# The first FFN product of chunks 2 to 8 by Strassen's scheme, with every operation of chunks 1 to 8 in a planned order

## The chip, the cores and the metric

The kernel runs on one core of one Trainium2 chip. The metric is the time of one execution in device microseconds, as a median over runs. Engines are named as in the profile: PE is TensorE (matmuls; PEld its weight loads), DVE is VectorE, ACT is ScalarE, POOL is GpSimd, SP is SyncE, which issues the DMA transfers.

## The reference

Attention over pooled keys and values, then a feed-forward network (FFN) with PReLU. There are 8 batches and 8 heads of 576 queries with 64 dimensions; keys and values are averaged over groups of 8, so 72 of each are left. The result is 4608 tokens of 512 features.

```python
k_p = k.reshape(B, H, Sp, pool, D).mean(axis=3)
v_p = v.reshape(B, H, Sp, pool, D).mean(axis=3)
scores = scale * np.matmul(q, k_p.transpose(0, 1, 3, 2))
scores = scores - np.max(scores, axis=-1, keepdims=True)
attn = np.exp(scores)
attn = attn / (np.sum(attn, axis=-1, keepdims=True) + 1e-09)
attn_out = np.matmul(attn, v_p)
...
h = x @ w_in
g = np.maximum(h, 0.0) + alpha * np.minimum(h, 0.0)
return (g @ w_out).astype(np.float32)
```

Here w_in is 512 x 2048 and w_out 2048 x 512.

## The kernel before

**Tiling.** The 4608 tokens are worked on in nine chunks of 512 (CH), numbered 0 to 8 here. A chunk has an attention part (`attention`) that makes its x, 512 features by 512 tokens, and an FFN part. Every fp32 operand of a matmul is split into a high and a low float16 part, and a product is the sum of three matmuls (low x high, high x low, high x high), which is why three lines stand side by side: L763 to L765 in the first FFN product, L810 to L812 in the second.

**The FFN of a chunk.** The first product (`ffn1_products`) makes 16 slices f of 128 hidden features each: 4 feature blocks of x times 3 matmuls of 128 x 128 weights and 512 columns, in one PSUM bank. Then ScalarE scales the slice from PSUM to SBUF (`ffn1_scaled`, L769), VectorE applies the PReLU (`ffn1_prelu`, L773; from chunk 1 on it reads SBUF alone, in chunk 0 it reads PSUM too), and the slice g is split: ScalarE writes the high part (L781) and GpSimd the low part (L784). The second product (`ffn2`) takes 128 tokens at a time: 16 slices times 3 matmuls of 512 columns in one bank, an output copy on ScalarE (L800) and a store on SP (L805). In the last tile of the last chunk the bank is made in two halves of 256 columns.

**The attention of a chunk.** Loads of q, k and v; group sums of k on VectorE (L374) and of v on GpSimd (three halvings, L461); maxima for the scales; splits of k, q and v; then for each of four tiles of 128 tokens: the scores on PE (L596), maximum and subtraction on VectorE (L505, L519), the exponential on ScalarE (L522), sum and reciprocal on VectorE, the product with the reciprocal on GpSimd (L530), the high part on ScalarE (L539, into a padded buffer `apad`), a copy of it by DMA (L536), two low parts on GpSimd (L542, L545) and a DMA transpose into `aT` (L550). After the four tiles the product with v, called mix (L606), gives x, which is split on ScalarE and VectorE (L564, L568).

**The order.** Chunk 0, the preparation of the weights and the attention of chunk 1 are ordered by `_Plan`: every operation is added with an engine, a duration, the operations that it needs, a rank and the buffers that it takes and gives, and `emit` writes out, again and again, the operation with the best rank among those that its engine could start soonest. From chunk 1 on the FFN operations are written down in a loop (L917 to L935), the attention of the next chunk is cut into portions that go between the 16 slices (`_Line`), and the Tile framework orders them. Buffers rotate: PSUM has two banks for slices (`ps_h`), two for outputs (`ps_o`) and two pairs for scores, mix and maxima (`ps_s`); in SBUF `fp` has four, `wp` three exponent buffers, `apads` two.

Of the kernel before, what the change touches and what calls it, by code (L numbers as in the profile page):

```python
# [7 lines left out]
F16 = mybir.dt.float16  # L8
# [24 lines left out]
LO0 = P - SP  # L33
TINY = 2.0 ** -100
# [38 lines left out]
class _Plan:  # L73

# [11 lines left out]
    def __init__(self, fill, **room):  # L86
        self.fill = fill
        self.ops, self.room, self.port = [], {k: n * [0.0] for k, n in room.items()}, 0.0

    def add(self, engine, us, emit, *after, rank=0.0, take=None, give=None, two=False):  # L90
        op = dict(engine=engine, us=us, emit=emit, after=after, rank=rank, n=len(self.ops),
                  take=take, give=(give,) if isinstance(give, str) else give or (), end=None,
                  two=two or engine == "Pool")
        self.ops.append(op)
        return op

    def start(self, op, free):
        if any(d["end"] is None for d in op["after"]) or (op["take"] and not self.room[op["take"]]):
            return None
        t = [free.get(op["engine"], 0.0)] + [d["end"] for d in op["after"]]  # L100
        if op["take"]:
            t.append(min(self.room[op["take"]]))
        if op["two"]:
            t.append(self.port)
        return max(t)

    def emit(self):
        free, left = {}, list(self.ops)
        while left:
            best = {}  # L110
            for op in left:
                t = self.start(op, free)
# [3 lines left out]
            for ready in best.values():  # L116
                t0 = min(t for t, _ in ready) + self.NEAR[ready[0][1]["engine"]]
                picks.append(min((x for x in ready if x[0] <= t0), key=lambda x: (x[1]["rank"], x[1]["n"])))
# [9 lines left out]
            if op["take"]:  # L128
                self.room[op["take"]].remove(min(self.room[op["take"]]))
            for kind in op["give"]:  # L130
                self.room[kind].append(op["end"])
            op["emit"]()
            left.remove(op)
# [3 lines left out]
def pooled_attention_prelu_ffn(ctx: ExitStack, tc: tile.TileContext, qT, kT, vT, kN, vN, w1, w2, alpha, out):  # L137
# [13 lines left out]
    atp = ctx.enter_context(tc.tile_pool(name="atp", bufs=1))  # L151
    xp = ctx.enter_context(tc.tile_pool(name="xp", bufs=4))
    fp = ctx.enter_context(tc.tile_pool(name="fp", bufs=ROOM["f"]))
    wp = ctx.enter_context(tc.tile_pool(name="wp", bufs=ROOM["e"]))
    gp = ctx.enter_context(tc.tile_pool(name="gp", bufs=16))
    ps_s = ctx.enter_context(tc.tile_pool(name="ps_s", bufs=2, space=PSUM))
    ps_h = ctx.enter_context(tc.tile_pool(name="ps_h", bufs=2, space=PSUM))
    ps_o = ctx.enter_context(tc.tile_pool(name="ps_o", bufs=2, space=PSUM))

    kbs = [const.tile([P, NPR, 2, SP], F16, name=f"kb{i}") for i in range(2)]  # L160
    apads = [const.tile([P, 2, H, P], F16, name=f"apad{i}") for i in range(2)]
    for i in range(2):
# [6 lines left out]
    nc.gpsimd.affine_select(out=ident, in_=ident, compare_op=ALU.not_equal, fill=1.0, base=0,  # L169
                            pattern=[[-1, P]], channel_multiplier=1)  # L170
# [21 lines left out]
    def reduce_max(add, r, m, n, *after, narrow=False, cap=None, rank=0.0):  # L192
# [7 lines left out]
        ps = once(lambda: ps_s.tile([P, 2, CH], F32, tag="s", name="pm"))  # L200
# [22 lines left out]
        return add("DVE", 0.4 + 0.13 * n, lambda: (maxima(), clamp()), *xs_, rank=rank, give="S")  # L223
# [78 lines left out]
    def attention(add, c, bs, rank, begin=False, early=False, k_pool=0, q_cuts=1, on_act=(), on_dve=(), behind=()):  # L302
# [99 lines left out]
        if first:  # L402
# [4 lines left out]
            def alpha_scales():  # L407
# [6 lines left out]
                nc.vector.tensor_scalar(out=xsc, in0=xsc, scalar1=2.0 ** -26, scalar2=None, op0=ALU.mult)  # L414
# [78 lines left out]
        for i in range(TPC):  # L493
# [40 lines left out]
            for l in range(2):  # L534
                if l and c > 1:
# [94 lines left out]
    def picked(f, n, of=NF):  # L630

        return (f + 1) * n // of > f * n // of
# [335 lines left out]
```

## Time and profile before

| | us |
|---|---|
| median of 3 runs | 872.73 (871.78 to 873.32) |
| the profiled execution's own time | 871.06 |
| its span, first to last instruction | 869.0 |
| PE busy in the span | 832.5 (96%) |
| DVE, ACT, POOL busy | 422.4, 408.8, 367.2 |

The profile is of one execution. Busy time counts instructions of an engine as the profiler sees them. Matmuls are pipelined: each is listed with 0.38 us, but the next one starts before it has ended, so what one costs is the distance between two starts. A row of the timeline has the start, the duration, the engine, the line of the program and, in square brackets, how long the engine was idle before and what ended that. A row of line groups has the busy time, the mean duration in ns, and the idle time before the group's instructions with what ended it.

### The profile page before, as it was taken

The page shows a single profiled execution, that of the slowest core. Times are in us where ns is not written, and L with a number is a line of the kernel's source. Part 1 is how long each engine was busy: PE and PEld are TensorE (multiplying, and loading weights), DVE is VectorE, ACT ScalarE, POOL GpSimd, SP SyncE. Part 2 cuts the span into 40 slices and gives each one's busy share as a digit, 9 for nine tenths or more (in the row PEclk, how much of TensorE's full clock was granted, in tenths as well). Part 3 has the DMA queues.
Part 4 walks back from the last instruction along what each step waited for, and adds up shares of the span by engine and source line. Part 5 has one row for each costly group of instructions (what it writes and reads, how often), then busy time and mean ns, then how long its engine had stood idle before and what let it go on. Part 6 is the DMA issues. An engine that isn't in the chain of part 4 may idle for free.

```text
span 869.0 us, 12499 instructions
## 1 busy us (share of the span) xinstructions
PE 832.5 (96%) x4941; PEld 397.1 (46%) x4941; DVE 422.4 (49%) x649; ACT 408.8 (47%) x692; POOL 367.2 (42%) x371
## 2 busy tenths in 40 slices
PE   6779899989999999999999999999999999999998
PEld 5444344434444444444444444444444444444445
DVE  4889995476129511872176208820782055112210
ACT  5999993545324531554155324632453255213330
POOL 0358473278215820683067406731573047103320
PEclk9999999999999999999999999999999999999999
DMA  9687042604710551047004701381126005100000
GB/s 341 228 249 293 26 105 51 206 4 78 202 52 5 100 179 43 13 84 196 30 23 74 210 25 28 64 196 48 28 55 146 13 20 94 36 25 13 1 24 25
DMA packets 122905, 78.92 MB, mean 91 GB/s; under 512 B 106176, under 2 KB 107008, under 8 KB 122848
## 3 DMA queue, kind: packets, MB, share of 16 engines
q1 hardware_dynamic: 122848, 78.14, 33.2%
q8 instruction: 38, 0.62, 0.3%
q14 instruction: 19, 0.16, 0.1%
HBM read 45.10 MB, written 9.44 MB: 63 GB/s over the span
## 4 chain that ended last, share of the span: by engine, by line
PE 70%; DVE 15%; ACT 6%; issue 3%; DMA 3%; POOL 2%; SPq 1%; ACTq 0%; POOLq 0%; DVEq 0%
PE o L810 13%; PE o L812 12%; PE o L811 12%; PE h L763 9%; PE h L764 9%; PE h L765 9%; DVE t L773 4%; DVE q L440 2%; PE x L606 2%; ACT t L769 2%; DMA qraw<-qT_dram 1%; PE idle L841 1%; DMA nat<-kN_dram 1%; POOL e L530 1%; DVE pr L215 1%
## 5 line engine op out<-in xcount | busy, mean ns | idle before, releaser
L784 POOL TENSOR_TENSOR g<-t,g 128x512 f16<-128x512 f32 x144 | 172.1, 1196 | 322.8 <-ACT g L781 322.8
L773 DVE SCALAR_TENSOR_TENSOR t<-t,al 128x512 f32<-128x512 f32 x128 | 127.1, 994 | 267.4 <-ACT t L769 259.3
L763 PE MATMUL h<-x,w 128*128 128x512 f16 x576 | 219.1, 380 | 11.7 <-ACT t L769 7.3
L764 PE MATMUL h<-x,w 128*128 128x512 f16 x576 | 219.0, 380 | 1.2 <-DVE x L568 1.1
L765 PE MATMUL h<-x,w 128*128 128x512 f16 x576 | 218.8, 380 | 0.0
L810 PE MATMUL o<-w,g 128*128 128x512 f16 (+1 forms) x560 | 208.1, 373 | 1.7 <-POOL g L784 0.9
L811 PE MATMUL o<-w,g 128*128 128x512 f16 (+1 forms) x560 | 208.8, 373 | 0.0
L812 PE MATMUL o<-w,g 128*128 128x512 f16 (+1 forms) x560 | 205.9, 373 | 0.0
L781 ACT CAST g<-t 128x512 f16<-128x512 f32 x144 | 88.6, 616 | 103.2 <-DVE t L773 102.8
L769 ACT ACTIVATE t<-h,rp 128x512 f32<-128x512 f32 x144 | 97.9, 681 | 68.6 <-PE h L765 60.6
L800 ACT ACTIVATE o<-o,os 128x512 f32<-128x512 f32 x33 | 22.5, 687 | 171.0 <-PE o L812 171.0
L764 PEld LDWEIGHTS <-w 128*128 128x128 f16 x576 | 56.4, 98 | 76.4 <-issue 14.7
L810 PEld LDWEIGHTS <-g 128*128 128x128 f16 x592 | 57.9, 98 | 68.7 <-POOL g L784 1.8
L812 PEld LDWEIGHTS <-g 128*128 128x128 f16 x592 | 57.9, 98 | 66.5
L461 POOL TENSOR_TENSOR vraw<-vraw 72x512 f32<-72x512 f32 (+1 forms) x56 | 56.4, 1023 | 75.3 <-DMA vraw<-vT_dram 66.6
L811 PEld LDWEIGHTS <-g 128*128 128x128 f16 x592 | 57.9, 98 | 66.0 <-issue 1.3
L765 PEld LDWEIGHTS <-w 128*128 128x128 f16 x576 | 56.5, 98 | 68.9 <-issue 2.6
L763 PEld LDWEIGHTS <-w 128*128 128x128 f16 x576 | 56.4, 98 | 65.5 <-issue 0.8
L568 DVE SCALAR_TENSOR_TENSOR x<-x,xsc,x 128x512 f16<-128x512 f32 x36 | 25.9, 748 | 79.1 <-ACT x L564 79.1
L530 POOL TENSOR_TENSOR e<-e,sm 128x576 f32<-128x576 f32 x35 | 43.8, 1252 | 21.9 <-DVE sm L528 20.7
L542 POOL TENSOR_TENSOR apad<-e,apad 128x448 f16<-128x448 f32 x36 | 39.2, 1090 | 8.1 <-ACT apad L539 8.1
L539 ACT CAST apad<-e 128x576 f16<-128x576 f32 x44 | 28.8, 669 | 22.9 <-POOL e L530 11.8
(131 smaller groups left out, 741.3 us busy)
## 6 DMA issues: line engine op xcount, KB each, us to landing
w<-w_dram SPq DMA_DIRECT2D x16, 1024.0 KB
out_dram<-o SPq DMA_DIRECT2D x35, 256.0 KB
qraw<-qT_dram SPq DMA_DIRECT2D x17, 512.0 KB
vraw<-vT_dram SPq DMA_DIRECT2D x28, 288.0 KB
kraw<-kT_dram SPq DMA_DIRECT2D x12, 576.0 KB
apad<-apad SPq DMA_DIRECT2D x28, 144.0 KB
kq<-kT_dram SPq DMA_DIRECT2D x2, 576.0 KB
nat<-kN_dram SPq DMA_DIRECT2D x2, 512.0 KB
```

The costliest lines, as they stand in the source:

```text
L461: nc.gpsimd.tensor_tensor(out=o, in0=y, in1=z, op=ALU.add)
L530: x = add("DVE" if i in on_dve else "Pool", us, lambda ex=ex, sm=sm, eng=eng: eng.tensor_tensor(out=ex(), in0=ex(), in1=sm().broadcast_to( ...
L763: nc.tensor.matmul(ps, w[:, 1, ks_], x[:, 0], start=(n == 0), stop=False)
L764: nc.tensor.matmul(ps, w[:, 0, ks_], x[:, 1], start=False, stop=False)
L765: nc.tensor.matmul(ps, w[:, 0, ks_], x[:, 0], start=False, stop=(n == NK - 1))
L769: nc.scalar.activation(t, hps[c, f], AF.Copy, scale=rp[:, f:f + 1])
L773: nc.vector.scalar_tensor_tensor(out=t, in0=t if c else h, scalar=(al if c else ra)[:, f:f + 1], in1=t, op0=ALU.mult, op1=ALU.max)
L781: nc.scalar.copy(out=g[:, 0], in_=t)
L784: nc.gpsimd.tensor_tensor(out=g[:, 1], in0=t, in1=g[:, 0], op=ALU.subtract)
L810: nc.tensor.matmul(ps, g[:, 1, ts_], w[:, 0, cs], start=(f == 0), stop=False)
L811: nc.tensor.matmul(ps, g[:, 0, ts_], w[:, 1, cs], start=False, stop=False)
L812: nc.tensor.matmul(ps, g[:, 0, ts_], w[:, 0, cs], start=False, stop=(f == NF - 1))
```

## The change

1. From chunk 2 on the first FFN product is made by Strassen's scheme (in the form with seven products and shared sums). x is cut into 2 x 2 blocks of 256 features by 256 tokens, and four slices f form a group d with their weights as 2 x 2 blocks. Seven products of 256 columns take the place of eight: 12 matmuls each, in three banks x, y, z that hold two 128-feature halves. VectorE adds the results out of the banks in SBUF (`plus`, five per group), ScalarE copies two. Scale, PReLU and split of g follow as before, all on SBUF.
2. The weight sums s1 to s4 that the scheme needs are made once, after the first product of chunk 1 (`sums`): PE adds high and low parts with an identity and a negative identity as stationary operand, VectorE and ScalarE add and split them again.
3. The input sums t1 to t4 and the splits of seven inputs are made per chunk at the end of `ahead`, which takes the place of `attention` from chunk 2 on. The mix is done in two halves of 256 tokens. The group sums of v are four VectorE reductions and no longer halvings on GpSimd.
4. All operations of chunks 1 to 8 go into the same `_Plan` (with named boxes for the buffers, `_Box`), and their order on every engine is the planner's. The buffers of the start are closed, and new ones are opened with fixed numbers: one pair of PSUM banks S for scores, mix and maxima, six single banks b for everything else; one exponent buffer, one `apad`, one half `aT`, one output buffer, two `ld` buffers for loads, four `h` buffers for slices.
5. In `reduce_max` each small PE product now also follows the one before it; two scale constants change by a factor of two.

```diff
+    def start(self, op):
+        t = [self.free.get(op["engine"], 0.0)]
+        t += [d["end"] + op["slack"] for d in op["after"] if self.loose < 1 or d["engine"] != op["engine"] or d["engine"] == "SP"]
...
-            xs_.append(add("PE", 0.15, lambda j=j, dg=dg: bring(j, dg), x, rank=rank, take=None if j else "S", give="d"))
+            xs_.append(add("PE", 0.15, lambda j=j, dg=dg: bring(j, dg), x, *xs_[-1:], rank=rank, take=None if j else home, give="d"))
...
+    homes = dict(
+        aT=[atp.tile([P, 2 * H, HC], F16, tag="aT", name="aT")],
+        f=[fp.tile([P, DM], F32, tag="f", name="f") for _ in range(2)],
+        o=[op_.tile([P, DM], F32, tag="o", name="o")],
+        e=[wp.tile([P, 2, 4, SP], F32, tag="e", name="e")],
+        h=[hp_.tile([P, 2, CH], F32, tag="h", name="h") for _ in range(4)],
+        xq=[xq.tile([P, 2, 2, HC], F16, tag="x16", name="x16") for _ in range(3)],
+        ld=[ldp.tile([P, KH], F32, tag="ld", name="ld") for _ in range(2)],
+        S=[ps_s.tile([P, 2, CH], F32, tag="s", name="s")],
+        b=[ps_b.tile([P, CH], F32, tag="b", name="b") for _ in range(6)],
...
+    def ahead(c, rank):
...
+                ps.append(add("DVE", 1.15, lambda i=i, t=t, vs=vs: nc.vector.tensor_reduce(
+                    out=vs()[:, 2 * i:2 * i + 2, :], in_=t(), axis=AX.X, op=ALU.add), x, *ps[-1:],
+                    take=() if i else vs, give=t))
...
+            x = add("PE", 0.56 * len(_parts(c, i)), lambda i=i, ps=ps: scores(c, i, ps()), *kd,
+                    qd[2 * (i // 2) + 1], *gate.get(c - 1, ()),
+                    take=(ps, ex), give=q16s[c][i // 2] if i % 2 else (), slack=FAR)
...
+            x = add("PE", 1.0, mixes, *td[2 * n:2 * n + 2], *vd, take=ps if n else (ps, X["b11"], X["b21"], F, G),
...
+        y = split("t2", [t2_], t2)
+        t4 = add("DVE", 0.72, lambda: nc.vector.tensor_tensor(out=f21(), in0=f21(), in1=t2(), op=ALU.subtract), t2_,
+                 two=True)
+        split("t1", [t1, t2_], f11)
+        split("t3", [t3, y], f12, give=G)
+        split("t4", [t4, hd["t1"]], f21, give=F)
...
+    def sums(i, used, rank):
...
+        def made(o, *terms):
+            for n, (t, m) in enumerate((t, m) for t, m in terms for _ in range(2)):
+                nc.tensor.matmul(o, m, a[t](n % 2), start=(n == 0), stop=(n == 2 * len(terms) - 1))
+        x = add("PE", 0.44, lambda: made(ps[0]()[:, 0], ((2, 1), ident), ((2, 2), ident)), *used,
+                take=ps, slack=FAR)
+        y = add("PE", 0.44, lambda: made(ps[1]()[:, 1], ((1, 1), ident), ((2, 1), minus)), x)
...
+    def fast(c, d, rank, *after):
+        banks = {n: _Box("b", halved) for n in "xyz"}
+        tall = [_Box("h") for _ in range(2)]
+
+        def product(bank, n, m, begin, end):
+            ps, x = banks[bank](), xs[c][m]()
+            for q in range(2):
+                for k in range(2):
+                    for e, (l, r) in enumerate(((1, 0), (0, 1), (0, 0))):
+                        nc.tensor.matmul(ps[:, q], weights(n, 2 * d + q, l, k), x[:, r, k],
+                                         start=begin and not (q or k or e), stop=end and q + k + e == 4,
+                                         skip_group_check=True)
+
+        def mul(n, bank, w, m, begin, *after):
+            end = d == NF // 4 - 1
+            return add("PE", 1.31, lambda: product(bank, w, m, begin, not begin and n != 4), xd[c][m], *after, *wd.get(d, ()),
+                       rank=rank + n, take=() if n > 2 else banks[bank], need=() if n else ("b", 3), slack=0.3, give=xs[c][m] if end else ())
...
+        def plus(bank, j, n, o=None):
+            z = half(j, n)
+            nc.vector.tensor_tensor(out=half(*o) if o else z, in0=banks[bank](), in1=z, op=ALU.add)
+
+        top, late = 1000 * c - 900, 1000 * c - 800 if d == NF // 4 - 1 else rank
...
+        p1 = mul(0, "x", "a11", "b11", True, *after)
+        p6 = mul(1, "y", "s2", "t2", True, p1)
+        p5 = mul(2, "z", "s1", "t1", True, p6)
+        a1 = add("ACT", 0.69, lambda: copy("x", 1), p1, rank=top, take=tall)
+        p2 = mul(3, "x", "a12", "b21", False, a1)
+        u2 = dve(lambda: plus("y", 1, 0, (0, 1)), p6, a1)
+        p7 = mul(4, "y", "s3", "t3", False, u2)
+        a2 = add("ACT", 0.69, lambda: copy("x", 0), p2, u2, rank=top, give=banks["x"])
+        u3 = dve(lambda: plus("y", 1, 0, (1, 1)), p7)
+        p4 = mul(5, "y", "a22", "t4", False, u3)
+        c22 = dve(lambda: plus("z", 1, 1), p5, u3)
+        p3 = mul(6, "z", "s4", "b22", False, c22)
+        c21 = dve(lambda: plus("y", 1, 0), p4, give=banks["y"])
+        c12 = dve(lambda: plus("z", 0, 1), p3, give=banks["z"])
...
+        blocks = [(i, d) for i in range(TPC) for d in range(NF // 4)] if done else [
+            (i, d) for ds, is_ in (((0, 1), (0, 1)), ((0, 1), (2, 3)), ((2,), range(4)), ((3,), range(4)))
+            for d in ds for i in is_]
...
+                    x = add("PE", 0.647 / halves, lambda i=i, n=n, f=f, cs=cs: step(i, n, f, cs), gd[c, f],
+                            *([last[i]] if i in last else [] if i < 2 or done else [begun[c]]),
...
+    used, begun, gate = {}, {}, {}
     for c in range(1, NC):
...
+        rank = 1000 * c
+        if c == 1:
+            for f in range(NF):
+                begun[1] = used[f] = plain(1, f, rank + 10 * f)
+        else:
+            for d in range(NF // 4):
+                begun[c] = fast(c, d, rank + 40 * d, *([begun[c]] if d else []))
+                if d == 2:
+                    gate[c] = [begun[c]]
+        ffn2(c, rank + 200)
+        if c == 1:
+            for d in range(NF // 4):
+                wd[d] = [x for q in range(2) for x in sums(2 * d + q, [begun[1]],
+                                                          rank - 300 + 10 * d + q)]
         if c + 1 < NC:
...
+            ahead(c + 1, rank - 500)
+    with tc.manual_schedule(engines={ENG.SP, ENG.PE, ENG.DVE, ENG.Activation, ENG.Pool}):
+        plan.emit()
```

## Rows read from the trace of the kernel before

**Rows 1.** The page: busy time by engine, and the chain that ended last.

```profile
PE 832.5 (96%) x4941; PEld 397.1 (46%) x4941; DVE 422.4 (49%) x649; ACT 408.8 (47%) x692; POOL 367.2 (42%) x371
...
PE 70%; DVE 15%; ACT 6%; issue 3%; DMA 3%; POOL 2%; SPq 1%; ACTq 0%; POOLq 0%; DVEq 0%
```

**Rows 2.** Stages: us, PE, PEld, DVE, ACT, POOL busy, clock, DMA, GB/s.

```profile
160.00:228.50 68.50, 64.69 (x403) 29.34 (x402) 38.13 (x58) 33.83 (x55) 42.11 (x41) 0.98 0.45 114
318.50:406.50 88.00, 87.75 (x517) 40.95 (x518) 42.76 (x61) 37.04 (x60) 40.16 (x41) 1.00 0.33 78
...
249.30:290.40 41.10, 39.31 (x293) 18.47 (x291) 29.82 (x46) 20.98 (x33) 23.04 (x25) 1.00 0.15 35
```

**Rows 3.** Waits of TensorE, 228 us to the end: total, times, longest.

```profile
PE h L763 <- ACT t L769: 4.4, 7, 1.5
PE o L810 <- ACT o L826: 0.6, 1, 0.6
PE o L810 <- ACT o L800: 0.2, 1, 0.2
```

**Rows 4.** Groups of lines, 228.5 to 318.5: busy, mean ns, idle before, releaser.

```profile
L763 PE MATMUL h<-x,w 128*128 128x512 f16 x64 | 24.3, 379 | 1.8 <-ACT t L769 1.8
```

**Rows 5.** Waits of TensorE, 100 to 230 us.

```profile
PE h L763 <- ACT t L769: 2.9, 1, 2.9
PE h L763 <- ACT o L800: 1.4, 1, 1.4
```

**Rows 6.** Timeline of TensorE, 178 to 192 us: start, us, what, idle before.

```profile
183.45 0.59 PE L763 MATMUL h<-x,w 128*128 128x512 f16 x1 [2.91 <-ACT t L769]
...
186.82 0.38 PE L765 MATMUL h<-x,w 128*128 128x512 f16 x1
...
191.29 0.56 PE L596 MATMUL s<-kb,q 64*128 64x72 f16 x24
```

**Rows 7.** Timeline of TensorE, 404 to 500 us.

```profile
404.56 1.97 PE L606 MATMUL x<-aT,v 88*64 88x256 f16 x32
...
406.69 0.38 PE L811 MATMUL o<-w,g 128*128 128x512 f16 x1
...
426.98 0.38 PE L812 MATMUL o<-w,g 128*128 128x512 f16 x1
```

**Rows 8.** Timeline of TensorE, 820 us to the end.

```profile
854.46 0.27 PE L810 MATMUL o<-w,g 128*128 128x256 f16 x1
...
858.71 0.27 PE L810 MATMUL o<-w,g 128*128 128x256 f16 x1
```

**Rows 9.** Groups of lines, whole span: busy, mean ns, idle before, releaser.

```profile
L784 POOL TENSOR_TENSOR g<-t,g 128x512 f16<-128x512 f32 x144 | 172.1, 1196 | 322.8 <-ACT g L781 322.8
L773 DVE SCALAR_TENSOR_TENSOR t<-t,al 128x512 f32<-128x512 f32 x128 | 127.1, 994 | 267.4 <-ACT t L769 259.3 <-issue 5.7 <-POOL g L784 2.0
...
L374 DVE TENSOR_REDUCE ks<-kraw 128x144 f32<-128x1152 f32 x12 | 15.7, 1346 | 2.4 <-DMA kraw<-kT_dram 2.4
...
L773 DVE SCALAR_TENSOR_TENSOR t<-h,m,t 128x512 f32<-128x512 f32 x16 | 11.9, 753 | 1.0 <-ACT t L769 1.0
```

**Rows 10.** Timeline of ScalarE, 260 to 320 us.

```profile
293.37 0.67 ACT L539 CAST apad<-e 128x576 f16<-128x576 f32 x1 [0.41 <-POOL e L530]
```

**Rows 11.** Timeline of VectorE, 260 to 320 us.

```profile
284.03 0.70 DVE L505 TENSOR_REDUCE mx<-s 128x8 f32<-128x576 f32 x1
...
291.96 0.71 DVE L505 TENSOR_REDUCE mx<-s 128x8 f32<-128x576 f32 x1
```

**Rows 12.** Timeline of GpSimd, 260 to 320 us.

```profile
295.86 0.43 POOL L545 TENSOR_TENSOR apad<-e,apad 128x128 f16<-128x128 f32 x1
...
301.47 0.88 POOL L545 TENSOR_TENSOR apad<-e,apad 128x128 f16<-128x128 f32 x1
```

**Rows 13.** Timeline of ScalarE, 195 to 230 us.

```profile
199.99 0.67 ACT L539 CAST apad<-e 128x576 f16<-128x576 f32 x1
...
208.62 0.67 ACT L539 CAST apad<-e 128x576 f16<-128x576 f32 x1 [1.30 <-DMA aT<-apad]
```

More of the change, by code (lines that the diff above doesn't have):

```diff
@@ L33 @@
 LO0 = P - SP
+KH = NPR * S // 2
 TINY = 2.0 ** -100
@@ L70, with __init__, __call__ @@
 ROOM = dict(d=3, big=12, f=4, e=3, v=3)
+class _Box:
+    def __init__(self, kind, view=None):
+        self.kind, self.view, self.slot = kind, view, None
+    def __call__(self):
+        return self.view(self.slot) if self.view else self.slot
 class _Plan:
@@ L107, in emit @@
     def emit(self):
-        free, left = {}, list(self.ops)
-        while left:
+        free, ops = self.free, self.ops
+        self.ops = []
+        wait, next_ = {}, {}
+        ready = []
+        for op in ops:
+            wait[op["n"]] = n = sum(d["end"] is None for d in op["after"])
+            for d in op["after"]:
+                if d["end"] is None:
+                    next_.setdefault(d["n"], []).append(op)
+            if not n:
+                ready.append(op)
+        while ready:
             best = {}
-            for op in left:
-                t = self.start(op, free)
+            for op in ready:
+                t = self.start(op)
                 if t is not None:
@@ L127, in emit @@
             op["end"] = t + op["us"] + (self.DMA_HOP if op["engine"] == "SP" else self.HOP)
[L128 to L131, printed above, removed]
-            op["emit"]()
-            left.remove(op)
+            for x in op["take"]:
+                some = self.room[getattr(x, "kind", x)]
+                slot = some.pop(min(range(len(some)), key=lambda n: some[n][0]))[1]
+                if isinstance(x, _Box):
+                    x.slot = slot
+            for x in op["give"]:
+                self.room[getattr(x, "kind", x)].append((op["end"], getattr(x, "slot", None)))
+            op["emit"]()
+            ready.remove(op)
+            for x in next_.get(op["n"], ()):
+                wait[x["n"]] -= 1
+                if not wait[x["n"]]:
+                    ready.append(x)
 @with_exitstack
@@ L915, in pooled_attention_prelu_ffn @@
[L915 to L935 removed]
+        return plan
@@ new lines, in pooled_attention_prelu_ffn, with parts, scaled_prelu @@
+    hb, ht, gd, xd, wd = {}, {}, {}, {}, {}
+    def parts(c, f, x, rank, give):
+        x = add("ACT", 0.62, lambda: ffn1_parts(c, f, 0), x, rank=rank, take="g")
+        gd[c, f] = add("Pool", 1.16, lambda: ffn1_parts(c, f, 1), x, rank=rank, give=give)
+    def scaled_prelu(t, f, scale, src=None):
+        if scale:
+            nc.scalar.activation(t, t if src is None else src, AF.Copy, scale=rp[:, f:f + 1])
+        else:
+            nc.vector.scalar_tensor_tensor(out=t, in0=t, scalar=al[:, f:f + 1], in1=t, op0=ALU.mult, op1=ALU.max)
@@ new lines, in plain, with products, scale @@
+    def plain(c, f, rank):
+        bank = _Box("b")
+        if f % 2 == 0:
+            ht[c, f // 2] = _Box("h")
+        pair = ht[c, f // 2]
+        def products():
+            hb[c, f] = bank()
+            for n in range(NK):
+                x, w, ks_ = xs[c][n](), w16[1][f], slice(n * P, n * P + P)
+                nc.tensor.matmul(hb[c, f], w[:, 1, ks_], x[:, 0], start=(n == 0), stop=False)
+                nc.tensor.matmul(hb[c, f], w[:, 0, ks_], x[:, 1], start=False, stop=False)
+                nc.tensor.matmul(hb[c, f], w[:, 0, ks_], x[:, 0], start=False, stop=(n == NK - 1))
+        def scale():
+            hs[c, f] = pair()[:, f % 2]
+            scaled_prelu(hs[c, f], f, True, hb[c, f])
+        y = add("PE", 2.59, products, rank=rank, take=bank,
+                give=[held("xp", x()) for x in xs[c]] if f == NF - 1 else ())
+        x = add("ACT", 0.7, scale, y, rank=rank - 900, take=() if f % 2 else pair, give=bank)
+        x = add("DVE", 0.7, lambda: scaled_prelu(hs[c, f], f, False), x, rank=rank - 900, two=True)
+        parts(c, f, x, rank - 900, pair if f % 2 else ())
+        return y
```

393 lines of the change are left out of this document (316 added, 77 removed).

## The prediction

> **What bounds the kernel now.** I began with the busy shares and the chain that ended last [rows 1]: TensorE is busy 96% of the span and makes up 70% of the chain, and VectorE, the next engine, is at 49%. Then the table by stage [rows 2]: in a whole middle chunk of 88.0 us TensorE is busy 87.75 us at full granted clock, VectorE 42.8, ScalarE 37.0, GpSimd 40.2. So a chunk lasts as long as its matmuls. TensorE's waits confirm it: from 228 us to the end only 5.2 us in all [rows 3], the most of it, 1.8 us, in the chunk of 228.5 to 318.5 [rows 4]. [...]
>
> What a matmul costs is the distance of starts, not its listed duration (0.38 us, pipelined). 94 starts of 512 columns take 20.29 us, 0.2159 each [rows 7]; 39 of 256 columns take 4.25 us, 0.1090 each [rows 8]. Half the columns cost half the time within 1%, though every one loads its own weights.
>
> **The parts.** The sum is made against the profiled execution's own 871.06 us (span 869.0 and 2.06 around it); the median of the runs is 872.73, 1.67 higher, and I carry each difference over to it.
>
> 1. *Products.* A chunk's first FFN product has 192 matmuls of 512 columns: 41.45 us. By Strassen's scheme it has 4 groups x 7 products x 12 matmuls of 256 columns, 336 x 0.1090 = 36.62. That is 4.83 us a chunk, and chunks 2 to 8 are seven: **-33.8**. TensorE is the bound, so all of it is on the path. (The first of the eight later chunks stays plain.)
>
> 2. *Weight sums.* Once, between the products of chunk 1 and chunk 2, 8 weight pairs get 8 matmuls of 256 columns each: 64 x 0.1090 = **+7.0**. Their VectorE steps (a pair has six of 256 columns and one of 512, at 0.38 and 0.75 by rows 9: 3.0 x 8 = 24 us) and the ScalarE copies lie under the second FFN product of chunk 1, 41.45 us of matmuls, and are costed at nothing; what the attention of chunk 2 needs of VectorE there beyond the other 17 would make the first groups of chunk 2 late, us for us.
>
> 3. *Mix by halves.* The attention's product with v covers the same columns in two halves; a chunk had 32 matmuls in 1.97 us [rows 7], 0.06 each, and most chunks now have 48 shorter ones. Bounds: nothing (columns equal) and 16 x 0.06 = 0.98 a chunk. I take 0.2, near the lower end because the columns are the same, x 7 = **+1.4**. The scores are unchanged.
>
> 4. *Old waits.* The 5.2 us of rows 3 belong to an order that no longer exists: **-5.2**; what waits in their place is part 6. In chunk 1 the product has six PSUM banks where it had two, so the 2.9 and 1.4 us waits for ScalarE to empty a bank go, and with them the slow matmuls: eight intervals took 3.37 us and would take 1.73. **-6.0**. Bounds: 0 and -11.2 for both.
>
> 5. *The other engines.* VectorE: 42.8 us a chunk, plus 20 additions from PSUM at 0.75 (as the PReLU that reads PSUM) [rows 9], 15.0, plus four v reductions in place of GpSimd's halvings, 1.35 x 1024/1152 = 1.20 each, 4.8, plus seven operations of 0.75 that form the split inputs where there were four, 2.3: 64.9 us of a chunk of about 84, 77%. ScalarE: 37.0, eight copies of 0.67 (as the pad copy) [rows 10] and, for the inputs, one of 1.1 and eight of 0.67 where there were four: 46. GpSimd: 40.2 and four more splits of 1.2 [rows 9] are 45.0 even before the halvings are taken off. None is above TensorE's 83, so they are hidden on average; the rivals are about where they are not. SP issues the same loads, pad copies, transposes and stores in a written order; a chunk's four output copies now share one buffer, so ScalarE stands before each until the store before it has landed, and what is queued behind it there, copies out of the banks, waits too. No row shows that wait; it is in the bounds of part 6. The order of the start is set by the same greedy rule with one new dependency among the small maximum products, which can shift it: 0 to +4, I take 0, because those products take part in few waits.
>
> 6. *New waits.* TensorE's queue is now a fixed list in which three of the seven products of a group wait for VectorE (a result must leave its bank before the next product adds to it), and the attention has one score bank pair, one exponent buffer, one padded buffer, half an aT. The later chunks show 5.2 / 7 = 0.74 us of waits on average and 1.8 at worst [rows 3, 4]. Bounds: 0 and 3 a chunk. I take the middle of mean and worst, 1.27, for there are more hand-overs: x 7 = **+8.9**.
>
> Sum: -33.8 + 7.0 + 1.4 - 5.2 - 6.0 + 8.9 = -27.7: 843.4 for the profiled execution, **845.0 for the median**.
>
> **Rivals.**
>
> *VectorE bounds the first product.* In the stage 249.3 to 290.4, the first product of chunk 2, VectorE is busy 29.8 of 41.1 us [rows 2]. With 15.0 of additions and 4.8 of v reductions it would have 49.6, and the stage shrinks to 36.6 of products plus at most 16 steps of the second product that may go ahead (3 x 0.216 each, 10.4): 47.0. The excess of 2.6 x 7 = 18 gives **863**. For it: the PReLU takes 994 ns from SBUF and 753 when it reads PSUM [rows 9], so it already loses time beside GpSimd's transfers. Against: additions read PSUM, outrank everything, and part of the attention's work can move to the second product's 41 us. Were the additions slowed as the PReLU is, 20 x 0.24 = 4.8 more a chunk and 34 in all, this rival would be at 897. Chance 0.14. [...]
>
> *The pause inside a group stays open.* After the product with s3, VectorE adds (0.75 and, by my estimate, 0.3 of hand-over) before the next may start in that bank: 1.05 us, unless the next group's first product, which needs three free banks of six, or a second-product step goes in. Left open in all 28 groups: 29.4 in place of 8.9, **865.5**. Against: banks are free until the second product takes its four. Chance 0.10.
>
> *The attention chain comes late: slower.* Scores of the next chunk may start only behind the third product of the third group. From there TensorE has 11 products (14.4), the second FFN product (41.45), four scores of 0.56 [rows 6], mix and one product (5.5): 61.4 us. One tile needs 12.3 us from its maximum at 284.03 to the end of its last pad write at 296.29 [rows 11, 12], 12.8 with scores; with single buffers four go one after the other, 51.2. From ScalarE's pad copy at 293.37, 2.9 before that end [rows 10], a transpose lands at most 8.6 later, by the copy that waits for it in the same buffer [rows 13]; then half a mix (1.0), two additions, a split on ScalarE and one on GpSimd, some 4.9 with hand-overs. Together 51.2 - 2.9 + 8.6 + 4.9 = 61.8, against 61.4: no slack by that tile, some 7 us by the other of those rows, which took 10.4 (291.96 to 302.35), 11.0 with scores. It decides through the steps of the second product done before the scores: each takes 0.65 of cover. With 8 of the 16 ahead the chain is 5.6 late, and 1.6 more is lost at the low clock as in rows 6: 7.2 x 6 changes of chunk = 43, **888**. It is slower from 4.9 us per change on. Against: the score operations outrank nearly all else. Chance 0.13.
>
> *The change doesn't do what it says:* the matmuls are counted in the loops, so the 33.8 can be given back but not missing. A worse start order and the rest: 0.03.
>
> **How the numbers follow.** The forecast's own case has 0.60: 834.7 (no new waits, no mix cost) to 857 (3 us of waits a chunk). A measurement of this kernel tells about 0.2% from no change, 871.0 to 874.5. Slower: the attention chain and half of the rest, 0.14. Same: 0.04, where a short form of the chain's lateness just eats the gain. Faster: 0.82. The range of 834 to 870 leaves out the late chain and the ends of the others, 0.2 at most.
>
> **What would show it.** Right: matmuls of the first product at 0.109 us from start to start, a middle chunk of about 84 us, TensorE over 95% busy at full clock, 64 sum matmuls in about 7 us around the end of chunk 1, VectorE near 65 us a chunk. The VectorE rival shows as matmuls that wait for additions while VectorE is over 95% busy; the open pause as about 1 us of idle in front of the sixth product of every group; the late chain as one long wait per chunk ahead of the second product of its first group, followed by starts 0.43 us apart for 512 columns, 0.21 for 256. A first product that starts late in chunk 2 alone speaks for the sums. I am wrong if the distance of 256-column starts is over 0.115, or if a middle chunk takes over 86 us.

## The result, and the profile after

The changed kernel takes **842.07 us** (median of 4 runs, 840.0 to 844.3) against 872.25 (871.09 to 873.32) for the kernel before on the same chip: a ratio of 0.9655, 95% interval 0.9625 to 0.9684. The forecast was 845.0. The profiled execution, the longest of the four, took 844.3 us, 842.6 of it span; before it was 871.06 and 869.0. So the median fell by 30.2 us and the profiled execution by 26.8. Where an experiment below names a time, it is a median. One execution of experiment 7 took 4255.31 us, for a reason that stays open, and is left out of its median.

The page, busy time by engine and the chain that ended last, to be read beside [rows 1]:

```profile
PE 805.7 (96%) x6073; PEld 501.1 (59%) x6073; DVE 549.2 (65%) x904; ACT 467.7 (56%) x807; POOL 345.7 (41%) x329
...
PE 82%; DVE 10%; DMA 4%; ACT 3%; issue 1%; SPq 0%; POOL 0%; ACTq 0%; DVEq 0%
```

TensorE is as full as before, and its share of the chain rose from 70 to 82%. VectorE has 127 us more to do (422.4 to 549.2) and yet is a smaller part of the chain. By stages, as in [rows 2] (us, then busy time of TensorE, its weight loads, VectorE, ScalarE, GpSimd, then granted clock, DMA share, GB/s): the first 156.2 us of the start (chunk 1 begins at 163.26), the first product of chunk 2, and two whole middle chunks:

```profile
0.00:156.20 156.20, 125.09 (x753) 64.32 (x755) 124.36 (x209) 121.21 (x231) 75.16 (x83) 0.91 0.59 190
...
259.00:306.50 47.50, 47.26 (x452) 37.76 (x450) 43.18 (x70) 29.23 (x49) 22.57 (x21) 1.00 0.38 103
343.00:426.00 83.00, 83.00 (x661) 54.79 (x660) 55.34 (x89) 43.08 (x71) 35.38 (x33) 1.00 0.39 88
426.00:509.60 83.60, 83.58 (x702) 55.20 (x701) 57.59 (x92) 45.21 (x75) 35.91 (x34) 1.00 0.36 88
```

A middle chunk takes 83.0 and 83.6 us where it took 88.0, and TensorE pauses in it for 0.02 us at most. In the 47.5 us of chunk 2's first product VectorE is busy 91%; over a whole chunk it is 67 to 69%. The granted clock is 1.00 from chunk 1 on, but 0.91 in the start.

TensorE's waits from 228 us to the end (total, times, longest), which answer to [rows 3]:

```profile
PE b L1309 <- ACT o L1315: 0.6, 1, 0.6
PE s L641 <- DVE sm L1090: 0.6, 1, 0.6
PE s L246 <- DVE x L1130: 0.3, 1, 0.3
```

That is 1.5 us in seven chunks, where there were 5.2. None of the three stands between a product and the addition that reads its bank. Why not, the timeline of TensorE shows, 378 to 396 us (start, us, line, what; L1252 is a product of the scheme, L1309 to L1311 the second FFN product, L631 the scores):

```profile
383.42 0.38 PE L1311 MATMUL b<-w,g 128*128 128x512 f16 x1
383.63 2.78 PE L1252 MATMUL b<-x,w 128*128 128x256 f16 x24
386.25 0.38 PE L1309 MATMUL b<-w,g 128*128 128x512 f16 x1
...
387.33 0.38 PE L1311 MATMUL b<-w,g 128*128 128x512 f16 x1
387.55 1.47 PE L1252 MATMUL b<-x,w 128*128 128x256 f16 x12
388.95 0.56 PE L631 MATMUL s<-kb,q 64*128 64x72 f16 x24
389.45 1.49 PE L1252 MATMUL b<-x,sw 128*128 128x256 f16 x12
390.77 0.38 PE L1309 MATMUL b<-w,g 128*128 128x512 f16 x1
```

After the 24 matmuls of two products there are six matmuls of the second FFN product from 386.25 to 387.55: 1.30 us, just where VectorE adds:

```profile
386.52 1.42 DVE L1269 TENSOR_TENSOR h<-b,h 128x512 f32<-128x512 f32 x2 [3.06 <-PE b L1252]
```

The first of these two additions reads the bank into which the matmuls from 387.55 on add. Six such steps stand in this place in the last group of each of the seven chunks. In the other 21 groups none does; there the next group's first products go in. In the first group of the chunk that begins at 343.11, the 36 matmuls below are the group's fourth and fifth products and the first of the next group; VectorE adds behind the fifth, and the group's sixth product follows at 352.39:

```profile
347.15 4.09 PE L1252 MATMUL b<-x,w 128*128 128x256 f16 x36
351.08 1.47 PE L1252 MATMUL b<-x,sw 128*128 128x256 f16 x12
352.39 1.47 PE L1252 MATMUL b<-x,w 128*128 128x256 f16 x12
```

```profile
350.04 1.41 DVE L1269 TENSOR_TENSOR h<-b,h 128x512 f32<-128x512 f32 x2
```

The 24 matmuls from 383.63 on took 2.62 us, 0.109 each, as in [rows 8].

### The profile page after: what moved, and what is told of

Read it like the earlier page. It is cut to its first block, busy times and chain, and to the rows that moved or that the text cites. A ratio compares the mean times of both kernels' runs of the same rounds, so it can differ in the third digit from the quotient of the medians.

```text
span 842.6 us, 15089 instructions
## 1 busy us (share of the span) xinstructions
PE 805.7 (96%) x6073; PEld 501.1 (59%) x6073; DVE 549.2 (65%) x904; ACT 467.7 (56%) x807; POOL 345.7 (41%) x329
## 4 chain that ended last, share of the span: by engine, by line
PE 82%; DVE 10%; DMA 4%; ACT 3%; issue 1%; SPq 0%; POOL 0%; ACTq 0%; DVEq 0%
PE b L1252 30%; PE b L1309 13%; PE b L1311 12%; PE b L1310 12%; PE s L631 2%; PE s L641 2%; DMA nat<-kN_dram 1%; DVE h L1217 1%; DVE m L279 1%; PE o L849 1%; PE o L850 1%; PE o L851 1%; DMA ld<-vT_dram 1%; PE h L850 1%; PE h L849 1%
## 5 line engine op out<-in xcount | busy, mean ns | idle before, releaser
L823 POOL TENSOR_TENSOR g<-h,g 128x512 f16<-128x512 f32 x128 | 159.8, 1265 | 202.1 <-ACT g L820 198.8
L1309 PE MATMUL b<-w,g 128*128 128x512 f16 (+1 forms) x528 | 197.2, 374 | 0.6 <-ACT o L1315 0.6
L1310 PE MATMUL b<-w,g 128*128 128x512 f16 (+1 forms) x528 | 196.9, 373 | 0.0
L1311 PE MATMUL b<-w,g 128*128 128x512 f16 (+1 forms) x528 | 196.9, 373 | 0.0
L1252 PE MATMUL b<-x,w 128*128 128x256 f16 x1344 | 156.9, 273 | 0.1
L1252 PEld LDWEIGHTS <-w 128*128 128x128 f16 x1344 | 130.6, 98 | 20.3 <-issue 0.5
L1269 DVE TENSOR_TENSOR h<-b,h 128x512 f32<-128x512 f32 x140 | 96.3, 688 | 51.0 <-PE b L1252 43.5
L1252 PE MATMUL b<-x,sw 128*128 128x256 f16 x1008 | 118.6, 273 | 0.0
L1217 DVE SCALAR_TENSOR_TENSOR h<-h,al 128x512 f32<-128x512 f32 x128 | 107.7, 870 | 9.6 <-ACT h L1215 9.6
L1215 ACT ACTIVATE h<-h,rp 128x512 f32<-128x512 f32 x112 | 76.2, 715 | 61.4 <-DVE h L1269 61.1
L1252 PEld LDWEIGHTS <-sw 128*128 128x128 f16 x1008 | 98.1, 98 | 11.5
L820 ACT CAST g<-h 128x512 f16<-128x512 f32 x128 | 77.3, 616 | 34.9 <-DVE h L1217 32.7
L1311 PEld LDWEIGHTS <-g 128*128 128x128 f16 x528 | 51.6, 98 | 59.0
L1309 PEld LDWEIGHTS <-g 128*128 128x128 f16 x528 | 51.6, 98 | 55.5 <-issue 1.8
L1134 POOL TENSOR_TENSOR x<-h,x 128x512 f16<-128x512 f32 x28 | 34.0, 1238 | 89.5 <-ACT x L1127 89.3
L1080 DVE TENSOR_REDUCE mx<-s 128x8 f32<-128x576 f32 x28 | 21.1, 752 | 30.4 <-PE s L631 30.2
```

The lines of the kernel that those rows point to most:

```text
L820: nc.scalar.copy(out=g[:, 0], in_=t)
L823: nc.gpsimd.tensor_tensor(out=g[:, 1], in0=t, in1=g[:, 0], op=ALU.subtract)
L1134: hd[n] = add("Pool", 1.15, lambda: nc.gpsimd.tensor_tensor(out=X[n]()[:, 1], in0=src(), in1=X[n]()[:, 0], op=ALU.subtract), h, give=give)
L1215: nc.scalar.activation(t, t if src is None else src, AF.Copy, scale=rp[:, f:f + 1])
L1217: nc.vector.scalar_tensor_tensor(out=t, in0=t, scalar=al[:, f:f + 1], in1=t, op0=ALU.mult, op1=ALU.max)
L1252: nc.tensor.matmul(ps[:, q], weights(n, 2 * d + q, l, k), x[:, r, k], start=begin and not (q or k or e), stop=end and q + k + e == 4, skip ...
```

## The experiments

Each starts from the changed kernel unless it says otherwise. The diffs show the edit alone.

### 1. The start as before (e1_start)

This touches only the start (chunk 0, the preparation of the weights and the attention of chunk 1): the new dependency among the small maximum products is left out there, which gives back the order of the start that the kernel before had.

```diff
-            xs_.append(add("PE", 0.15, ..., x, *xs_[-1:], ...))
+            xs_.append(add("PE", 0.15, ..., x, *(() if home == "S" else xs_[-1:]), ...))
```

> The changed kernel, with the one new dependency of the small maximum products taken out for the start alone, so that the start is written in the order of the kernel before. Theory (the start's order costs 9 us): the last matmul of chunk 0 comes back from 163.3 to about 154.5 us and the time falls by 5 to 9 us, to 833 to 838. Rival (the closed buffers of the start or the negative identity made on GpSimd slow it): the last matmul of chunk 0 stays near 163 and the time stays at 840 to 844.

Measured: 838.63 us (837.42 to 839.49), ratio 0.9625 (0.9604 to 0.9647). That is 3.4 us below the changed kernel, less than the 5 to 9 expected, and the fastest version that leaves nothing out. The intervals of the two ratios overlap, but each of the five runs lies below each of the four of the changed kernel (840.0 and more). The stretch in which most of it is won, 80 to 120 us, of the changed kernel:

```profile
80.00:120.00 40.00, 31.57 (x196) 14.41 (x194) 37.30 (x54) 33.95 (x58) 21.32 (x19) 0.88 0.26 98
```

and of this one:

```profile
80.00:120.00 40.00, 35.40 (x251) 16.38 (x250) 38.17 (x62) 37.44 (x80) 21.30 (x19) 1.00 0.32 111
```

In the same 40 us 251 matmuls run in place of 196, and at the full clock. The two longest groups of TensorE's waits in the changed kernel, up to 156 us; the second is one wait of the scores for a VectorE step, and ends at 114.62:

```profile
PE pm L246 <- ACT pd L243: 8.2, 6, 2.8
PE s L631 <- DVE q L479: 5.7, 1, 5.7
```

Of the first line 3.1 us are left in this kernel, of the second 0.3. So the dependency that should cost nothing does cost: 3.4 us in the medians, 5.7 between the two profiled spans (842.6 and 836.9). Chunk 1 itself starts 7.5 us earlier (155.76, not 163.26, and 155.84 before); 3.2 of them are lost again in chunk 1, where one maximum product waits 2.30 us for ScalarE and eight matmuls behind it start 0.43 us apart.

### 2. The planned order without Strassen's scheme (e2_plain)

Chunks 2 to 8 keep the list scheduler and its fixed buffers, but take the plain first product: 192 matmuls of 512 columns, and the plain split of its input.

```diff
-        X = xs[c] = {n: _Box("xq" if n in ("t2", "t3", "t4") else "xp", fine) for n in (...)}
+        X = xs[c] = [_Box("xp") for _ in range(NK)]
...
-            split("b11", ...), split("b21", ...), split("b22", ...), split("t1", ...) ...
+            for j in range(NK):
+                h = add("ACT", 0.45, ...)
+                y.append(add("DVE", 0.42, ...))
```

> The planned order without Strassen's scheme: chunks 2 to 8 get 192 matmuls of 512 columns, as in chunk 1, and no weight sums. Theory (a chunk lasts as long as its matmuls, the planner only removes waits): 842 + 7 x 4.83 - 7.0 = 869, a middle chunk of 88.3 us. Rival (the new order itself brings the gain): 850 or less, a middle chunk of 85 or less.

Measured: 887.83 us (885.95 to 888.11), ratio 1.0188 (1.0166 to 1.021): slower than before, where I expected a gain of some 3 us. The waits of TensorE from 228 us:

```profile
PE s L246 <- DVE x L1126: 14.1, 5, 3.4
PE b L1284 <- ACT o L1290: 0.6, 1, 0.6
```

and one of the five on the timeline:

```profile
438.10 0.37 PE L246 MATMUL s<-pd,ones 128*128 128x128 bf16 x2 [2.81 <-DVE x L1126]
438.27 0.63 PE L1204 MATMUL b<-x,w 128*128 128x512 f16 x1
438.69 0.63 PE L1205 MATMUL b<-x,w 128*128 128x512 f16 x1
```

In five of the seven chunks the small maximum product, which has its fixed place in the list and needs the one score bank, waits until VectorE has split the last input out of that bank; every product stands in the queue behind it. Behind this one seven starts lie 0.42 us apart, and 12 and 9 behind the first and the last of the five. That is the distance of the slow starts of [rows 6]: in the trace of the kernel before, the granted clock is 0.50 over those, 183.45 to 186.82 us, and 1.00 right behind them, to 190 us. Starts twice as far apart are called the lower clock below, too. Over 438.10 to 530.50 us, which holds these seven starts, the granted clock is 0.98 on average, where it is 1.00 over 347.40 to 438.10. From chunk 2's first product on (254.30) the execution takes 632.1 us, where it took 619.8 from 249.19 before: +12.3. The last four waits (10.7), some 28 starts late by 0.21 (5.9) and the 0.6, less the 5.2 of old waits that are gone, are 12.0. The other 5.1 of the 17.4 between the spans lie ahead of 254.30. So the planned order of the plain product gains nothing. The changed kernel is 887.83 - 842.07 = 45.8 us faster; 33.8 - 7.0 = 26.8 of that are matmuls, and the other 19.0 are about what this wait and the slow starts cost here (14.1 and 5.9), of which the changed kernel has 0.3 left. But the planner orders the two kernels differently, so this run alone doesn't part the scheme from its order.

### 3. More work for VectorE (e3_dve)

```diff
+                x = add("DVE", 0.7, lambda f=f: nc.vector.tensor_tensor(out=hs[c, f], in0=hs[c, f], in1=hs[c, f], op=ALU.max),
+                        x, rank=late, two=True)
```

> One more VectorE operation of 512 columns ahead of each PReLU of chunks 2 to 8, which leaves the values as they are: 16 a chunk, some 12 us, so VectorE goes from 57 to about 69 of 84 us. Theory (TensorE is the bound with VectorE well below): at most 1 us a chunk, under 850. Rival (VectorE is nearly the bound of the first product: it is busy 43.2 of 47.5 us there): 12 minus 4 of slack a chunk, 7 x 8, about 895.

Measured: 903.95 us (900.57 to 907.33), ratio 1.0378: the theory's "under 850" is refuted, and the rival's 895 is near. The added operation, from 250 to 850 us:

```profile
L1297 DVE TENSOR_TENSOR h<-h 128x512 f32<-128x512 f32 x103 | 84.6, 821 | 1.6 <-ACT h L1215 1.6
```

16 x 0.82 = 13.1 us a chunk. TensorE's waits from 250 us, the longest groups:

```profile
PE b L1252 <- ACT h L1265: 13.0, 7, 5.1
PE s L631 <- DVE pt L249: 8.1, 2, 7.8
PE b L1252 <- ACT x L1127: 7.5, 5, 2.0
PE b L1252 <- POOL x L1134: 6.1, 5, 1.3
```

Over 350 to 440 us VectorE is busy 70.7 of 90, 79%, and the kernel is already 62 us slower. Most of the waits name ScalarE or GpSimd; that VectorE's delay reaches TensorE by way of the copies and splits that follow it is likely, but not shown. Of the 92 us added in seven chunks 62 came through, some of them as low clock (0.96 granted over 350 to 440 us, where it was 1.00). So an engine with a third of its time free on average took in only a third of the work. That the stage (91%, above) and the order count and not the mean is the reading that fits; the new operation also changed the planner's order, and this run doesn't part the two.

### 4. The scores of the next chunk one group later (e4_gate3)

```diff
-                if d == 2:
+                if d == 3:
```

> Scores of the next chunk may start behind the third product of the last group and no longer of the third: 9.2 us less cover for the attention chain. In the changed kernel the second mix comes 60 us after that point's scores began and its inputs are ready about 2 us before they are used. Theory (the chain has hardly any slack): 7 us late in each of 6 changes of chunk and 1.6 at the low clock, about 890. Rival (the tiles are far apart only because nothing is urgent): under 850.

Measured: 884.03 us (883.13 to 884.92), ratio 1.0149. TensorE's waits from 250 us:

```profile
PE b L1252 <- ACT x L1127: 14.7, 6, 3.5
PE b L1252 <- POOL x L1134: 7.4, 6, 1.3
PE s L246 <- DVE x L1130: 4.5, 1, 4.5
```

One group is 7 x 12 x 0.109 = 9.2 us less of cover, and a change of chunk then waits 4.2 to 4.8 us, 4.4 on average (mostly 3.0 to 3.5 and 1.2 to 1.3; the last line is the same lateness at another place). So by this run the chain had about 9.2 - 4.4 = 4.8 us to spare, an estimate that takes the two as one for one. The trace of the changed kernel shows less: the second product of a chunk reads a split (t2) that GpSimd ended 1.3 to 4.1 us before it, at the closest at 426.11 for a start at 427.43. At 437.57, behind two such waits of 3.15 and 1.27 us, 11 matmuls took 2.30 us, 0.21 each and not 0.109, the lower clock. This is the picture that the prediction drew for the late chain, one long wait per chunk ahead of the second product of the first group and slow matmuls behind it, and 884 is near the 888 that it gave. The mechanism is real, and the change stays between 1 and 5 us on the right side of it.

### 5. Without the weight sums (e5_nosums)

```diff
-        if n in ("s1", "s2"):
-            return sw[i // 4][:, i % 4, l, HC * (n == "s2"):HC * (n == "s2") + HC][:, cs]
...
+        j, h = dict(a11=(0, 0), a12=(0, 1), a22=(1, 1), s3=(1, 0), s1=(0, 0), s2=(0, 1), s4=(1, 1))[n]
...
-                wd[d] = [x for q in range(2) for x in sums(2 * d + q, [begun[1]], ...)]
+                wd[d] = []
```

> Left out: the weight sums; the products that use them read plain weights of the same shape instead. Theory (64 matmuls of 256 columns on a bound engine, their VectorE steps hidden): 7.0 us less, about 835. Rival (the sums' VectorE steps delay chunk 2 as well): 10 us less or more. Other rival (they lie in waits): no change.

Measured: 850.33 us (848.79 to 851.5), ratio 0.9746 (0.9721 to 0.977): 8 us **slower** than with the sums, which neither the theory nor its rivals had. Chunk 2's first product did start earlier, at 250.1 instead of 259.0. But the scheduler, given other work around chunk 1, chose another order for everything behind it: the first products of chunks 2 to 8 start 85.2, 81.9, 89.6, 81.9, 87.7 and 89.5 us apart. TensorE's waits from 240 us:

```profile
PE b L1248 <- ACT x L1127: 5.8, 3, 2.3
PE b L1248 <- POOL x L1134: 4.5, 4, 1.4
```

They stand at changes of chunk, with the releasers of experiment 4. They add up to 10.3 us. The four long chunks exceed 83.5 by 18.0 in all, and the two short ones fall below it by 3.2; not all of that is resolved. So this run didn't price the sums, since it changed two things; experiments 8 and 9 do.

### 6. The pause inside a group left open (e6_open)

Each group's first product now waits for the last product of the group before it, and every tile's second FFN product for the last product of the chunk's last group, so that none of its steps may fill the pause.

```diff
-                             *([last[i]] if i in last else [] if i < 2 or done else [begun[c]]),
+                             *([last[i]] if i in last else [begun[c]]),
...
-                begun[c] = fast(c, d, rank + 40 * d, *([begun[c]] if d else []))
+                begun[c], last_p = fast(c, d, rank + 40 * d, *([last_p] if d else []))
```

> A group's first product may start only behind the last product of the group before, and no step of the second product before the first one has ended, so that nothing can fill the pause while VectorE adds. Theory (the pause of about 1 us in each of the 28 groups is there and is filled by other matmuls): 28 x 1.05 more and something at the ends of the groups, 870 to 885. Rival (the additions are done in time without any filling): under 850.

Measured: 881.65 us (880.75 to 882.54), ratio 1.0106. TensorE's waits from 250 us:

```profile
PE b L1252 <- DVE h L1269: 25.5, 28, 1.6
PE s L246 <- DVE e L1082: 5.6, 2, 3.8
```

28 waits, one for each group, of 0.91 us on average, where I had worked out 1.05. The pause exists, and the changed kernel, whose waits above have none of this kind, fills all 28. With the smaller waits, which come from the other order, TensorE waits 34.8 us from 250 us on; the spans differ by 36.4 (879.0 and 842.6). One pause and what follows it on the timeline:

```profile
366.10 1.47 PE L1252 MATMUL b<-x,w 128*128 128x256 f16 x12 [0.86 <-DVE h L1269]
367.41 0.82 PE L1252 MATMUL b<-x,sw 128*128 128x256 f16 x6
```

12 matmuls in 1.31 us, 0.109 each, and a granted clock of 1.00 over 343 to 426 us: the clock doesn't fall behind this pause, and behind the other 27 (0.8 to 1.6 us) the next twelve matmuls start 0.11 us apart as well.

### 7. No gate at all (e7_nogate)

```diff
-                if d == 2:
+                if d == 9:
```

> Scores may start as soon as their inputs are there, with no wait for the third group. Theory (TensorE has no waits to lose): 842 within 3 us. Rival (the earlier softmax takes VectorE from the additions in the first product): 850 or more. If the chain of the attention had cost time: less than 838.

Measured: 844.77 us (843.1 to 845.56), ratio 0.968 (0.9656 to 0.9704), whose interval overlaps that of the changed kernel. With the gate a group later the time rose by 42 us, without it by 2.7, which is not clear of noise. So the gate isn't what makes the kernel fast; it only must not come late.

### 8 and 9. More and fewer sum matmuls in an unchanged order (e8_sums2, e9_sums1)

Both start from experiment 1. The planned durations, and so the order, are the same in all three.

```diff
-            for n, (t, m) in enumerate((t, m) for t, m in terms for _ in range(2)):
-                nc.tensor.matmul(o, m, a[t](n % 2), start=(n == 0), stop=(n == 2 * len(terms) - 1))
+            for again in range(2):
+                for n, (t, m) in enumerate((t, m) for t, m in terms for _ in range(2)):
+                    nc.tensor.matmul(o, m, a[t](n % 2), start=(n == 0), stop=(n == 2 * len(terms) - 1))
```

> e1_start's kernel (838.63 us) with every group of matmuls that makes a sum of two halves of the first product's weights issued twice over (the second pass starts the bank anew, so the values are the same): 64 more matmuls, 0.109 us each, the planned order of all work otherwise the same. Theory that TensorE's own time is the bound and that the sums cost what their matmuls take: +7.0 us, 844 to 847. Rival, that the sums lie in TensorE's pauses of chunks 0 and 1 and that leaving them out gained nothing for that reason: within 2 us of 838.6.

```diff
-            for n, (t, m) in enumerate((t, m) for t, m in terms for _ in range(2)):
-                nc.tensor.matmul(o, m, a[t](n % 2), start=(n == 0), stop=(n == 2 * len(terms) - 1))
+            nc.tensor.matmul(o, terms[0][1], a[terms[0][0]](0), start=True, stop=True)
```

> e1_start's kernel (838.63 us) with one matmul in place of four in each group that makes a sum of two halves of the first product's weights, so the products of chunks 2 to 9 run on a part of the weights' sums: 48 matmuls fewer, 0.109 us each, the planned order of all work otherwise the same. Theory that the sums cost what their matmuls take, and that the kernel without sums lost its gain to another order: -5.2 us, 831.5 to 835. Rival, that the sums lie in pauses anyway: within 2 us of 838.6.

Measured: 843.95 us (841.84 to 845.2; ratio 0.9682, 0.9662 to 0.9702) with twice the matmuls, and 834.84 (833.45 to 838.42; 0.9589, 0.9566 to 0.9613) with a quarter of them: +5.3 and -3.8 against 838.63, a little less than the +7.0 and -5.2 expected. The first is clear of noise; the ratio's interval of the second overlaps that of experiment 1. The traces are sharper. The end of the sums' stage is the first product of chunk 2, in experiment 1, at

```profile
254.67 1.47 PE L1252 MATMUL b<-x,w 128*128 128x256 f16 x12
```

and in experiment 8, with one of its first groups of sum matmuls above it:

```profile
200.86 1.26 PE L1185 MATMUL b<-w,ident 128*128 128x256 f16 x10
...
260.35 1.47 PE L1253 MATMUL b<-x,w 128*128 128x256 f16 x12
```

From the first sum matmul to there it is 52.51 us in experiment 1 (from 202.16), 59.49 in experiment 8 (+7.0) and 48.19 in experiment 9 (from 202.33 to 250.52, -4.3, with a new wait of 0.36 in it). So the 64 matmuls do cost 7.0 us, and the order, not the sums, is what made experiment 5 slow. The profiled execution of experiment 9 keeps nothing of its 4.3: new waits from there on, the longest 1.8 us, take it back (spans 836.7 and 836.9); its other three runs were 833.45 to 834.92.

## Why the prediction was right

The time was forecast at 845.0 and is 842.07, inside the range and by the mechanism that was named: TensorE's own time is the bound and Strassen's scheme shortens it. Its terms were not all right, though. I split the profiled executions at the first product of chunk 2 (249.19 before, 258.98 after) and where chunk 1's product could begin (154.46 before, its first matmul at 155.84 less the 1.38 that this waited for a bank; 163.26 after).

**From chunk 2 on** the forecast was -33.8 + 1.4 - 5.2 + 8.9 = -28.7. Measured: 619.8 us became 583.6, **-36.2**.

- *Part 1, products*: held. The matmuls of 256 columns start 0.109 us apart, and from first product to first product the six chunks 2 to 7 take 83.5 us on average where they took 88.7.
- *Part 4, old waits of these chunks*: they are gone, -5.2, though experiment 2 shows that the new order alone has worse ones.
- *Part 6, new waits*: mis-sized. I took "the middle of mean and worst, 1.27" a chunk, +8.9, "for there are more hand-overs"; the new waits are 1.5 us in all. The reason that I gave against the open pause, that other work goes in, applied here as well, and I counted it there only. Experiment 6 shows the size of what is filled: 28 x 0.91.
- *Part 3, mix*: held, though not tried alone. From its first matmul to what follows, a chunk's mix took 1.91 us; its two halves take 1.01 to 1.06 each, so 0.15 more a chunk, where 0.2 was forecast. With 1.5 in place of 8.9 the four terms make -36.1, the measured sum within 0.1.

**Chunk 1** was to change by +7.0 - 6.0 = +1.0; it took 94.7 us before and 95.7 after, **+1.0**.

- *Part 2, sums*: 7.0 by the stages of experiments 1 and 8. In the changed kernel one pair's eight matmuls stand closely packed among the others (the timeline of TensorE at 206 us), with no wait around them:

```profile
206.47 0.82 PE L1184 MATMUL b<-w,ident 128*128 128x256 f16 x6
207.13 0.38 PE L1184 MATMUL b<-w,minus 128*128 128x256 f16 x2
207.35 0.82 PE L1184 MATMUL b<-w,ident 128*128 128x256 f16 x6
208.00 0.38 PE L1184 MATMUL b<-w,minus 128*128 128x256 f16 x2
```

  (two pairs, 0.88 us each: 8 x 0.109).
- *Part 4, chunk 1's waits and low clock*: 1.0 - 7.0 = -6.0, as forecast from the two waits of [rows 5] and the slow starts of [rows 6]. TensorE's waits in chunk 1 are 0.7 us in all, and the granted clock there is 1.00, where it was 0.98.

**The start** was costed at 0 with bounds of 0 to +4, "because those products take part in few waits". It was longer by **+8.8** in the profiled execution, of which experiment 1 gives back 7.5, and 3.4 in the medians of the whole kernel. This step failed: those products' own waits for ScalarE grew from 2.8 to 8.2 us, the scores behind them waited 5.7 us for VectorE, and the granted clock of the start fell from 0.98 to 0.91. The three stages add up to -36.2 + 1.0 + 8.8 = -26.4, the difference of the spans. So two terms were wrong by 7.4 and 8.8 us, in opposite directions; the forecast of -27.7 owes its closeness to that, which is luck.

**Part 5, the other engines.** VectorE was put at 64.9 us a chunk and is busy 55 to 58 in the three middle chunks from 343.0 to 593.2 us, 48 in the two behind them. The additions take 688 ns, not 750 (page, costliest groups), and chunks 2 to 7 hold 16 v reductions, not four in each:

```profile
L1269 DVE TENSOR_TENSOR h<-b,h 128x512 f32<-128x512 f32 x140 | 96.3, 688 | 51.0 <-PE b L1252 43.5
L1217 DVE SCALAR_TENSOR_TENSOR h<-h,al 128x512 f32<-128x512 f32 x128 | 107.7, 870 | 9.6 <-ACT h L1215 9.6
```

The PReLU from SBUF takes 870 ns on average where it took 994 [rows 9], but its median is 743 and its longest 1697, and each of the 28 over 800 ns ran beside a GpSimd instruction; the 61 that ran beside none took 735 to 753. In the kernel before it was the same: the 46 beside none took 733 to 752 ns, and each of the 60 over 800 ran beside one. Of the 16 that read PSUM there, nine ran beside one and took 774 at most. The additions, which have one input in PSUM, took 675 to 693 ns each, also the 69 that ran beside one, so they were not slowed as the PReLU is, by the 0.24 us each with which the VectorE rival would have stood at 897. ScalarE's wait for the shared output buffer, for which the prediction had no row, is 14.9 us in eight waits in the trace of the changed kernel, the longest 4.8.

**The rivals.** *VectorE as the bound* did not decide, but stood close: 43.2 us of 47.5 in the first product of chunk 2, where 49.6 were forecast, and experiment 3 shows what 13 us more would do. *The open pause* is priced by experiment 6, at 0.91 us of wait each: 0.69 of addition and 0.22 of hand-over, where the prediction put 0.3 without a row for it. The changed kernel fills it. *The late chain* was put between no slack and 7 us; experiment 4 makes it about 4.8 and the trace 1.3 to 4.1, and its consequence, 884 with one group less, is as drawn. *The change not doing what it says* is excluded by the counts: L1252 has 2352 matmuls (1344 and 1008), 7 x 336.

## What to carry to other kernels

When the bounding engine is full, what an algorithm saves on it arrives in full where each new hand-over has other work of that engine to stand in it, as it had here (left open, the hand-overs took 25.5 us); so count the hand-overs and name what fills each, rather than adding a flat allowance for waits. A greedy order is a part of the kernel: leaving 7 us of work out made it 8 us slower, and one extra dependency ahead of the changed part cost some 3, so after any change of a planner's input read every stage, also those that were not meant to change. To price a piece of work inside a planned order, repeat or thin it with the order kept, and don't remove it from the plan.

## What was not expected of the hardware

The clock. In experiment 2 five waits of the same kind were followed by different clocks. The line at 438.10 above is followed by starts 0.43 us apart, this one, as long, by starts 0.216 apart:

```profile
530.53 0.27 PE L246 MATMUL s<-pd,ones 128*128 128x128 bf16 x2 [2.81 <-DVE x L1126]
530.64 0.38 PE L1204 MATMUL b<-x,w 128*128 128x512 f16 x1
530.85 0.38 PE L1205 MATMUL b<-x,w 128*128 128x512 f16 x1
```

In all: behind 3.41 us (at 254.1) and 2.81 (at 438.1) 12 and 7 matmuls of 512 columns started 0.43 us apart, behind 2.11 and again 2.81 (at 347.4 and 530.5) all started 0.216 apart, and behind 2.97 (at 621.5) the first two did and the next nine did not. So the length of a wait alone doesn't say whether the clock falls; what else decides stays open here. Behind the 28 pauses of 0.8 to 1.6 us in experiment 6 it didn't fall. And a start whose engines are equally busy (VectorE 124.4 us, ScalarE 121.2, where they were 124.9 and 123.6) lost clock, 0.91 against 0.98 before, by a changed order of small products alone: experiment 1, which takes back only that, has 0.98 again.
